# Rearranging the first two attentions of an attention-and-experts kernel

## The chip, the cores and the metric

The kernel runs on one core of a Trainium2 chip. A core has five engines that run side by side and wait for each other through semaphores: TensorE (matmuls; PE in the profile, PEld for its weight loads), VectorE (DVE), ScalarE (ACT), GpSimd (POOL) and SyncE (SP, which here only starts transfers). Each engine takes its own instructions in program order, so an instruction that has to wait holds up everything behind it on that engine, and nothing on the others. The metric is the time of one execution on the device in microseconds (us). Before the change it is 366.86 us, the median of three runs from 366.44 to 367.07.

## What is computed

Eight batches of grouped attention are followed by a mixture of experts with a two-level gate. Cut to what matters:

```python
# q (8, 16, 384, 64), k and v (8, 4, 384, 64), all float32
k = np.repeat(k, 4, axis=1); v = np.repeat(v, 4, axis=1)
scores = 1/np.sqrt(64) * np.matmul(q, k.transpose(0, 1, 3, 2))
attn = np.exp(scores - np.max(scores, axis=-1, keepdims=True))
attn = attn / (np.sum(attn, axis=-1, keepdims=True) + 1e-09)
x = np.matmul(attn, v)                       # then reshaped to (3072, 1024)

g_logits = x @ w_group                       # 4 groups
g_idx = np.argmax(g_logits, axis=1)          # and its softmax weight g_w
for g in range(4):
    e_logits = xg @ w_expert[g]              # 4 experts in each group
    e_idx = np.argmax(e_logits, axis=1)      # and its softmax weight e_w
    for e in range(4):
        h = np.maximum(xg[mask_e] @ w1[g, e], 0.0)
        ye = h @ w2[g, e]
        out[tok_idx] = (g_w * e_w)[:, None] * ye
```

## The kernel before

The kernel goes through the batches one after another. It guesses, from the mean of v, which expert the batch will choose, fetches the weights of that expert early, and runs the batch through it. The gate then says which tokens did choose it; a loop at the end does whatever was missed. The attention of batch b + 1 overlaps the expert of batch b.

An attention has 4 groups (g) of 6 units (c), so 24 units (u). TensorE does the score matmuls of unit u + 2, then the value matmuls of unit u; ScalarE takes the exponential of each unit's scores from PSUM into a buffer `e` (13 of them go round). To get the sums of the exponentials, GpSimd adds units 0 and 1 and units 2 and 3 of each group, in place, and VectorE reduces what is left (`reduce`, four times a group). When a group is done its output is copied from PSUM to `xT`.

```python
        def add(self, eng, u):
            eng.tensor_add(out=self.e[u], in0=self.e[u], in1=self.e[u + 1])

        def reduce(self, g, n, u):

            def emit():
                if reds[self.b] is None:
                    reds[self.b] = gpool.tile([P, Hkv, NR, 2, NB], F32, name="red")
                nc.vector.tensor_reduce(
                    out=reds[self.b][:, g, n].rearrange("p t j -> p (t j)"),
                    in_=self.e[u].rearrange("p t (j x) -> p (t j) x", x=32),
                    axis=AX.X, op=ALU.add, apply_transpose=True)
            if self.held is None:
                emit()
            else:
                self.held.append(emit)

        def release(self):
            for emit in self.held:
                emit()
            self.held = None

        def tail(self, u):
            b = self.b
            g, c = u // NC, u % NC
            z = u - c
            if c in (1, 3) and (b, u) != (1, 3):
                self.add(nc.gpsimd, u - 1)
            if (b, g) == (2, 0):
                for n in ((), (1,), (2, 0))[max(c, 3) - 3]:
                    self.reduce(g, n, (z, z + 4, z + 5)[n])
            elif c >= 3:
                self.reduce(g, c - 3, (z, z + 4, z + 5)[c - 3])
            if c == NC - 1:
                self.reduce(g, NR - 1, z + 2)
                if b not in xT:
                    # ... (makes xT[b]; for batch 1 in the room of a weight tile)
                dst, src = xT[b][:, KG * g:KG * (g + 1), :], self.oT[g][:, :, :S]
                if b > 1 and g < Hkv - 1 or (b, g) == (1, 1):
                    nc.vector.tensor_copy(out=dst, in_=src)
                else:
                    nc.scalar.copy(out=dst, in_=src)

        def run(self, u0, u1, inserts, nxt=None):
            for u in range(u0, u1):
                if u + 2 < NU:
                    self.score(u + 2)
                elif nxt is not None:
                    nxt.score(u + 2 - NU)
                self.pv(u)
                self.tail(u)
                for f in inserts.get(u, []):
                    f()
```

`collect` puts the four partial sums of a group together, `sums` sends them through TensorE to a PSUM tile and takes the reciprocal of what comes back, `spread` brings the reciprocals to the layout of `xT`, `scale_x` multiplies, and `cast` makes the bfloat16 copy that the expert reads. The PSUM tile "x" is the one of the two "o" tiles that the running group does not use; the next group takes it.

```python
    def collect(b, g0, g1):
        if b not in rsum:
            rsum[b] = gpool.tile([P, Hkv, 2, NB], F32, name="rsum")
        nc.vector.tensor_reduce(
            out=rsum[b][:, g0:g1].rearrange("p g t j -> p g (t j)"),
            in_=reds[b][:, g0:g1].rearrange("p g n t j -> p g (t j) n"), axis=AX.X, op=ALU.add)

    def sums(b, g0, g1, pt):
        if isinstance(pt, str):
            pt = ps_tile(pt)
        sm = pt[:, 1, 128:128 + Hkv * KG * NB].rearrange("p (g r j) -> p g r j", r=KG, j=NB)
        for r in range(2):
            for t in range(2):
                nc.tensor.matmul(out=sm[t * D:(t + 1) * D, g0:g1, r, :], lhsT=half32[:, r, :],
                                 rhs=rsum[b][:, g0:g1, t, :], start=True, stop=True)
        if b not in inv:
            inv[b] = gpool.tile([P, KQ, NB], F32, name="inv")
        nc.vector.reciprocal(out=inv[b][:, KG * g0:KG * g1],
                             in_=sm[:, g0:g1].rearrange("p g r j -> p (g r) j"))

    def spread(b, m, which=None):

        rb = gpool.tile([P, 2, S], F32, name="rb", bufs=2) if which is None else ps_tile(which)[:, :, :S]
        for r in range(2):
            nc.vector.transpose(
                out=rb[:, r].rearrange("p (j x) -> p j x", x=32),
                in_=inv[b][:, 2 * m + r].unsqueeze(2).to_broadcast([P, NB, 32]))
        return rb

    def scale_x(b, m, rb, eng):
        # ... (makes xb[b])
        x = xT[b][:, 2 * m:2 * m + 2, :]
        eng.tensor_mul(out=x, in0=x, in1=rb)

    def normalise(b, m, which=None):
        scale_x(b, m, spread(b, m, which), nc.vector)

    def cast(b, m, eng=None):
        ks = slice(2 * m, 2 * m + 2)
        evac(eng or nc.scalar, xb[b][:, ks, :], xT[b][:, ks, :])
```

The guess needs the sum of v over the positions (`sum_v`: one reduction on VectorE, or three additions on GpSimd), then a mean and two small matmuls, a chain of small VectorE operations that picks the expert (`pick_index`, cut here), and a read of the index into a GpSimd register (`pick`):

```python
    def sum_v(b, eng):
        vsum[b] = gpool.tile([P, Hkv, D], BF16, name="vsum")
        # on VectorE: one tensor_reduce over the positions of vraw[b] (line 461)
        # on GpSimd: three tensor_adds, 768, 256 and 256 wide (lines 467 to 469; in the diff)

    def pick_index(b):
        # ...
        nc.vector.tensor_scalar(oh1, key, km, None, op0=ALU.is_ge)     # line 580
        # ...

    def pick(b):
        ers[b] = nc.gpsimd.value_load(e_is[b][0:1, 0:1], min_val=0, max_val=NE - 1)

    def pick_w1(b):
        w1s[b] = fetch1(ers[b])

    def pick_w2(b):
        w2s[b] = fetch2(ers[b])

    # ffn_h: 16 matmuls for 256 columns of the hidden layer (in the diff)

    def first_fetch():
        pick(0)
        transposed(1)
        pick_w1(0)
```

The schedule of the first two attentions lists what is put in after which unit. `hold` keeps back the reductions of attention 1 until `release`:

```python
    GB = KG * SC
    a = at[0]
    a.run(0, NU, {
        1: [do(first_q, GB, GB, "x", nc.vector)],
        3: [cast_k],
        4: [gate_matrix_b, do(sum_v, 0, nc.gpsimd)],
        6: [do(collect, 0, 0, 1)],
        7: [do(first_q, 2 * GB, 2 * GB, "x", nc.vector)],
        8: [do(first_k, 1, "x", nc.vector)],
        10: [do(sums, 0, 0, 1, "x"), do(normalise, 0, 0)],
        13: [first_guess],
        14: [do(cast, 0, 0)],
        15: [do(collect, 0, 1, 2), first_pick],
        19: [first_fetch, do(sums, 0, 1, 2, "x")],
        20: [first_spread],
        21: [first_scale],
    }, at[1])
    collect(0, 2, Hkv)

    FU = 16
    a = at[1]
    hold(a)
    a.run(0, FU, {
        4: [do(sums, 0, 2, Hkv, "x")],
        5: [second_scale, do(a.add, nc.gpsimd, 2), do(pick_w2, 0), do(sum_v, 1, nc.vector)],
        6: [do(normalise, 0, 3, "x")],
        9: [do(load_k, 2), do(load_q, 2), do(cast, 0, 2)],
        11: [a.release, do(collect, 1, 0, 2), do(cast, 0, 3)],
    })
    moe_h(0, 0, "s")        # first of four expert tiles of batch 0
    # ... the rest of this stretch is in the diff
    a.run(FU, NU, {21: [do(sum_v, 2, nc.gpsimd)]})

    def first_block():
        prefetch(1)
        collect(1, 2, Hkv)
        weights[0]()
        out_weights(0)
        cast(1, 0)
        cast(1, 1)
        moe_y(0, 0, "s")
        sums(1, 2, Hkv, "o")
        normalise(1, 2)
        normalise(1, 3)
        moe_y(0, 1, "s")
        cast(1, 2)
        # ... rest of batch 0, then attention 2
```

Of the kernel before, what the change touches and what calls it, by code (L numbers as in the profile page):

```python
# [18 lines left out]
def kernel(  # L19
# [11 lines left out]
    nc = tc.nc  # L31
# [262 lines left out]
    class Attn:  # L294
# [62 lines left out]
        def tail(self, u):  # L357
            b = self.b
            g, c = u // NC, u % NC
            z = u - c  # L360
            if c in (1, 3) and (b, u) != (1, 3):
                self.add(nc.gpsimd, u - 1)
            if (b, g) == (2, 0):
                for n in ((), (1,), (2, 0))[max(c, 3) - 3]:
                    self.reduce(g, n, (z, z + 4, z + 5)[n])
            elif c >= 3:
                self.reduce(g, c - 3, (z, z + 4, z + 5)[c - 3])
            if c == NC - 1:
                self.reduce(g, NR - 1, z + 2)
                if b not in xT:  # L370
                    if b == 1:
                        w = wpool.tile([P, KQ, F], BF16, name="w1")
                        xT[b] = w.rearrange("p a f -> p (a f)").bitcast(F32)[
                            :, :KQ * S].rearrange("p (a n) -> p a n", n=S)
                    else:
                        xT[b] = xpool.tile([P, KQ, S], F32, name="xT", bufs=1)
                dst, src = xT[b][:, KG * g:KG * (g + 1), :], self.oT[g][:, :, :S]
                if b > 1 and g < Hkv - 1 or (b, g) == (1, 1):
                    nc.vector.tensor_copy(out=dst, in_=src)  # L379
                else:  # L380
                    nc.scalar.copy(out=dst, in_=src)  # L381

# [71 lines left out]
    vsum = {}  # L454

    def sum_v(b, eng):

        vsum[b] = gpool.tile([P, Hkv, D], BF16, name="vsum")
        with nc.allow_low_precision("only serves a guess"):
            if eng is nc.vector:  # L460
# [3 lines left out]
            n = NC // 2 * D  # L464
            t = gpool.tile([P, 2, S], F32, name="rb", bufs=2).rearrange(
                "p a s -> p (a s)").rearrange("p (g n) -> p g n", g=Hkv)
            eng.tensor_add(out=t, in0=vraw[b][:, :, :n], in1=vraw[b][:, :, n:])
# [150 lines left out]
    def ffn_h(x, w1, hT, f0, which, mid=None):  # L618
        h = ps_tile(which)
        for jj in range(2):  # L620
            for kq in range(KQ):
                nc.tensor.matmul(out=h[:, jj, :S], lhsT=w1[:, kq, (f0 + jj) * P:(f0 + jj + 1) * P],  # L622
                                 rhs=x[:, kq, :], start=(kq == 0), stop=(kq == KQ - 1))
            if mid is not None and jj == 0:
                mid()
# [23 lines left out]
    def moe_h(b, f0, which, mid=None):  # L649
        if f0 == 0:  # L650
            hTs[b] = xpool.tile([P, FQ, S], BF16, name="hT", bufs=1)
        ffn_h(xb[b], w1s[b], hTs[b], f0, which, mid)
# [48 lines left out]
    def first_fetch():  # L701
        pick(0)
        transposed(1)
        pick_w1(0)
# [21 lines left out]
    def second_scale():  # L726
# [7 lines left out]
        4: [gate_matrix_b, do(sum_v, 0, nc.gpsimd)],  # L734
# [3 lines left out]
        10: [do(sums, 0, 0, 1, "x"), do(normalise, 0, 0)],  # L738
        13: [first_guess],
        14: [do(cast, 0, 0)],  # L740
        15: [do(collect, 0, 1, 2), first_pick],
        19: [first_fetch, do(sums, 0, 1, 2, "x")],
# [9 lines left out]
        4: [do(sums, 0, 2, Hkv, "x")],  # L752
        5: [second_scale, do(a.add, nc.gpsimd, 2), do(pick_w2, 0), do(sum_v, 1, nc.vector)],
        6: [do(normalise, 0, 3, "x")],
        9: [do(load_k, 2), do(load_q, 2), do(cast, 0, 2)],
        11: [a.release, do(collect, 1, 0, 2), do(cast, 0, 3)],
    })
    moe_h(0, 0, "s")
# [4 lines left out]
    guess_mean(1, pt)  # L763
    vm = mean_copy(pt, nc.scalar)
    moe_h(0, 2, "s", do(sums, 1, 0, 2, pt))
    guess_logits(vm, pt)
    for m in range(2):
        normalise(1, m)
    moe_h(0, 4, "s")
    weights[0] = gate_softmax(0, pt, True)  # L770
    pick_index(1)
    moe_h(0, 6, "s")
    a.run(FU, NU, {21: [do(sum_v, 2, nc.gpsimd)]})

    def first_block():

        prefetch(1)
        collect(1, 2, Hkv)
# [212 lines left out]
```

The softmax here doesn't subtract the row's maximum and nothing guards it: scores larger than these inputs give would overflow.

## Time and profile before

| | before |
|---|---|
| time, median of 3 runs | 366.86 us |
| span of the profiled execution | 366.1 us |
| mean granted TensorE clock | 0.998 |
| TensorE / VectorE / ScalarE / GpSimd busy | 354.2 / 275.7 / 230.2 / 160.5 us |

The stretch that the change touches, from the table of busy time in stretches of 10 us (TensorE, VectorE, ScalarE and GpSimd, in us of 10):

| us | PE | DVE | ACT | POOL |
|---|---|---|---|---|
| 0 to 10 | 8.46 | 5.12 | 5.54 | 6.38 |
| 10 to 20 | 9.88 | 6.46 | 7.80 | 8.40 |
| 20 to 30 | 9.17 | 9.56 | 8.89 | 7.54 |
| 30 to 40 | 8.47 | 9.31 | 8.17 | 7.86 |
| 40 to 50 | 9.13 | 9.93 | 9.18 | 9.09 |
| 50 to 60 | 10.00 | 8.71 | 2.34 | 5.42 |
| 60 to 70 | 9.81 | 8.72 | 7.08 | 4.35 |
| 70 to 80 | 10.00 | 7.38 | 5.52 | 6.11 |

Attention 0 runs from about 7 to 33 us, units 0 to 15 of attention 1 from there to 50, the first half of batch 0's expert to 62.7, and the last 8 units of attention 1 to 69.4.

In the lines of a timeline the columns are the start, the time from start to end of the piece, the engine, the kernel's line, the operation, what it writes and reads with shapes, and how many instructions stand in the piece. In brackets behind it is the idle time of that engine ahead of the piece and what ended it. In the list of waits a line gives the engine and line that waited, what it waited for, and the total, the number and the longest of these waits. TensorE's matmuls overlap, and their ends are modelled, so starts are the safer thing to read.

### The profile page before, as it was taken

What the parts mean: (1) busy time and instruction counts of PE and PEld (TensorE: products, weight loads), DVE (VectorE), ACT (ScalarE), POOL (GpSimd) and SP (SyncE); (2) the same over time, 40 slices, a digit from 0 to 9 for tenths busy, and PEclk for the clock granted to TensorE, in tenths of its full rate; (3) what the DMA queues carried; (4) which work ended last, traced back from release to release, by engine and by line L of the source; (5) the groups of instructions that cost most, each with busy time, mean ns of one, the idle gap of its engine ahead of it and who ended that gap; (6) DMA issues with size and microseconds to landing.
All of it is one profiled execution on the core that took longest, in us unless ns stands there. A gap on an engine that the chain in (4) does not pass through costs nothing.

```text
span 366.1 us, 9424 instructions
## 1 busy us (share of the span) xinstructions
PE 354.2 (97%) x3907; PEld 183.2 (50%) x3907; DVE 275.7 (75%) x506; ACT 230.2 (63%) x300; POOL 160.5 (44%) x127
## 2 busy tenths in 40 slices
PE   8999899999999999999999999999999999999992
PEld 4544455445455455554455445554545545555641
DVE  5689998858988498867989579884998659892230
ACT  5789853759926597267954599265972679544221
POOL 6886890736811476033730377113760258300000
PEclk9999999999999999999999999999999999999999
DMA  8973999999998999999999999989999899999333
GB/s 188 251 118 57 194 181 220 156 208 253 224 163 173 216 252 211 148 209 238 232 208 148 205 249 212 192 175 216 252 210 137 151 211 234 212 213 240 90 85 93
DMA packets 69902, 69.79 MB, mean 191 GB/s; under 512 B 35832, under 2 KB 49944, under 8 KB 69856
## 3 DMA queue, kind: packets, MB, share of 16 engines
q0 software_dynamic: 26864, 41.81, 65.1%
q1 hardware_dynamic: 42320, 26.40, 31.2%
q10 hardware_dynamic: 672, 0.93, 0.9%
q8 instruction: 32, 0.52, 0.5%
q14 instruction: 14, 0.11, 0.1%
HBM read 89.21 MB, written 12.58 MB: 278 GB/s over the span
## 4 chain that ended last, share of the span: by engine, by line
PE 87%; DVE 5%; ACT 2%; POOL 1%; issue 1%; DMA 1%; ACTq 0%
PE ps_o L329 28%; PE ps_s L622 22%; PE ps_s L633 13%; PE ps_s L310 8%; PE ps_o L633 7%; PE ps_o L451 3%; DVE red L343 3%; ACT e L316 2%; PE ps_s L896 2%; PE ps_o L622 1%; POOL e L336 1%; PE ps_o L896 1%; DMA w<-in_q_dram 1%; PE ps_o L415 1%; DVE rb L426 1%
## 5 line engine op out<-in xcount | busy, mean ns | idle before, releaser
L316 ACT ACTIVATE e<-ps_s 128x768 f32<-128x768 f32 x192 | 150.7, 815 | 20.1 <-PE ps_s L310 16.2
L329 PE MATMUL ps_o<-e,v_raw 64*64 64x384 f32 x1536 | 153.3, 483 | 1.4 <-DVE inv L419 1.4
L336 POOL TENSOR_TENSOR e<-e 128x768 f32<-128x768 f32 x64 | 116.4, 1836 | 62.6 <-ACT e L316 43.8
L343 DVE TRANSPOSE_TENSOR_REDUCE red<-e 128x24 f32<-128x768 f32 x128 | 114.1, 946 | 18.3 <-POOL e L336 18.3
L622 PE MATMUL ps_s<-xb,w 128*128 128x384 bf16 x480 | 81.0, 326 | 0.5 <-ACT e L316 0.5
L329 PEld LDWEIGHTS ps_o<-e,v_raw 64*64 64x64 f32 x1536 | 55.4, 133 | 39.7 <-issue 27.4
L622 PEld LDWEIGHTS <-w 128*128 128x128 bf16 x512 | 48.9, 98 | 36.2 <-issue 4.7
L310 PE MATMUL ps_s<-qT,kT 64*64 64x384 bf16 x768 | 63.7, 326 | 0.7 <-ACT e L316 0.2
L626 ACT ACTIVATE hT<-ps_s 128x768 bf16<-128x768 f32 x30 | 24.3, 811 | 61.0 <-PE ps_s L622 58.0
L633 PE MATMUL ps_s<-w,hT 128*128 128x512 bf16 x224 | 50.6, 379 | 0.0
L633 PEld LDWEIGHTS <-hT 128*128 128x128 bf16 x336 | 31.3, 97 | 36.6 <-issue 2.1
L310 PEld LDWEIGHTS <-kT 64*64 64x64 bf16 x768 | 24.2, 105 | 38.9 <-issue 37.1
L689 POOL COPY after<-qT 128x1 bf16<-128x1 bf16 x7 | 2.1, 304 | 79.5 <-DMA qT<-q_raw 78.1
L426 DVE STREAM_TRANSPOSE rb<-inv 128x384 f32<-128x384 f32 x62 | 32.0, 555 | 0.4
L658 ACT ACTIVATE ot<-ps_s,we 128x1024 f32<-128x1024 f32 x14 | 15.6, 1115 | 25.5 <-PE ps_s L633 12.1
L633 PE MATMUL ps_o<-w,hT 128*128 128x512 bf16 x112 | 26.5, 379 | 0.0
L435 DVE TENSOR_TENSOR xT<-xT,rb 128x768 f32<-128x768 f32 x25 | 24.0, 958 | 0.9
L245 ACT CAST xb<-xT 128x768 bf16<-128x768 f32 x27 | 21.7, 830 | 0.0
L461 DVE TENSOR_REDUCE vsum<-v_raw 128x256 bf16<-128x1536 f32 x6 | 16.9, 2815 | 0.0
L379 DVE COPY xT<-ps_o 128x768 f32<-128x768 f32 x18 | 16.5, 919 | 0.0
L660 DVE TENSOR_SCALAR ot<-ps_o,we 128x1024 f32<-128x1024 f32 x7 | 9.0, 1282 | 5.6 <-PE ps_o L633 4.6
L381 ACT COPY xT<-ps_o 128x768 f32<-128x768 f32 x10 | 8.0, 799 | 6.6 <-PE ps_o L329 6.6
(129 smaller groups left out, 201.4 us busy)
## 6 DMA issues: line engine op xcount, KB each, us to landing
w<-in_moe_w_dram POOLq DMA_DIRECT2D x16, 2048.0 KB, 23.4
out_dram<-ot SPq DMA_DIRECT2D x42, 256.0 KB, 6.6
q_raw<-in_q_dram POOLq DMA_DIRECT2D x7, 768.0 KB, 32.1
v_raw<-in_v_dram SPq DMA_DIRECT2D x12, 384.0 KB, 5.3
k<-in_k_dram POOLq DMA_DIRECT2D x7, 192.0 KB, 28.9
out_dram<-ot SPq DMA_DIRECT2D x7, 128.0 KB, 2.3
v_raw<-in_v_dram POOLq DMA_DIRECT2D x2, 384.0 KB, 11.5
w<-in_q_dram POOLq DMA_DIRECT2D x3, 192.0 KB, 7.5
```

The lines of the kernel that those rows point to most:

```text
L245: eng.copy(out=out_, in_=in_)
L310: nc.tensor.matmul(out=sT[r * H2:(r + 1) * H2, s, :S], lhsT=kT[b][s * D:(s + 1) * D, slot, ks], rhs=qT[b][s * D:(s + 1) * D, kq * SC:(kq + ...
L316: nc.scalar.activation(e.rearrange("p t (s x) -> p s t x", s=2), sT[:, :, :S].rearrange("p s (t x) -> p s t x", t=2), ACT.Exp, scale=scale)
L329: nc.tensor.matmul(out=oT[t * D:(t + 1) * D, r, :S], lhsT=vraw[b][r * H2:(r + 1) * H2, g, c * D:(c + 1) * D], rhs=self.e[u][r * H2:(r + 1) ...
L336: eng.tensor_add(out=self.e[u], in0=self.e[u], in1=self.e[u + 1])
L343: nc.vector.tensor_reduce(out=reds[self.b][:, g, n].rearrange("p t j -> p (t j)"), in_=self.e[u].rearrange("p t (j x) -> p (t j) x", x=32) ...
L426: nc.vector.transpose(out=rb[:, r].rearrange("p (j x) -> p j x", x=32), in_=inv[b][:, 2 * m + r].unsqueeze(2).to_broadcast([P, NB, 32]))
L435: eng.tensor_mul(out=x, in0=x, in1=rb)
L461: eng.tensor_reduce(out=vsum[b], in_=vraw[b].rearrange("p g (c d) -> p g d c", d=D), axis=AX.X, op=ALU.add)
L622: nc.tensor.matmul(out=h[:, jj, :S], lhsT=w1[:, kq, (f0 + jj) * P:(f0 + jj + 1) * P], rhs=x[:, kq, :], start=(kq == 0), stop=(kq == KQ - 1))
L626: nc.scalar.activation(hT[:, f0:f0 + 2, :], h[:, :, :S], ACT.Relu)
L633: nc.tensor.matmul(out=y[:, nh, :], lhsT=hT[:, f, c * P:(c + 1) * P], rhs=w2[:, f, nh * HALF:(nh + 1) * HALF], start=(f == 0), stop=(f == ...
```

## The change

It rearranges the work of the engines beside TensorE in attentions 0 and 1; the matmuls are the same in number and shape. Batch 0's sum of v on GpSimd is cut in two, so that additions of exponentials come between its parts; batch 1's goes from VectorE to GpSimd, behind the last additions ahead of the expert. The index of batch 0's expert is read ahead of the addition of units 18 and 19. The PSUM copies of attention 0's group 3 and attention 1's groups 0 and 2 go from ScalarE to VectorE, and in group 1 of attention 1 the copy goes ahead of the reductions. The last three reductions of group 2 in attention 1 are done at the pause for the expert, as their exponentials are there by then. The reductions of attention 1 are released after unit 8 in place of 11. Two casts leave the run of exponentials; they now come ahead of the first expert tile, whose matmuls are reordered to read the parts of `x` in the order in which they become ready. Sums, mean and guess of batch 1 come one expert tile later, and its `pick_index` after attention 1.

```diff
@@ -357,16 +357,12 @@
         def tail(self, u):
             b = self.b
             g, c = u // NC, u % NC
-            z = u - c
-            if c in (1, 3) and (b, u) != (1, 3):
+            if c in (1, 3):
                 self.add(nc.gpsimd, u - 1)
-            if (b, g) == (2, 0):
-                for n in ((), (1,), (2, 0))[max(c, 3) - 3]:
-                    self.reduce(g, n, (z, z + 4, z + 5)[n])
-            elif c >= 3:
-                self.reduce(g, c - 3, (z, z + 4, z + 5)[c - 3])
+            sums_first = (b, g) != (1, 1)
+            if sums_first or c < NC - 1:
+                self.reductions(g, c)
             if c == NC - 1:
-                self.reduce(g, NR - 1, z + 2)
                 if b not in xT:
                     if b == 1:
                         w = wpool.tile([P, KQ, F], BF16, name="w1")
@@ -375,10 +371,25 @@
                     else:
                         xT[b] = xpool.tile([P, KQ, S], F32, name="xT", bufs=1)
                 dst, src = xT[b][:, KG * g:KG * (g + 1), :], self.oT[g][:, :, :S]
-                if b > 1 and g < Hkv - 1 or (b, g) == (1, 1):
+                if b > 0 and g < Hkv - 1 or (b, g) == (0, Hkv - 1):
                     nc.vector.tensor_copy(out=dst, in_=src)
                 else:
                     nc.scalar.copy(out=dst, in_=src)
+                if not sums_first:
+                    self.reductions(g, c)
+
+        def reductions(self, g, c):
+
+            b, z = self.b, g * NC
+            if (b, g) == (1, 2) and c > 3:
+                return
+            if (b, g) == (2, 0):
+                for n in ((), (1,), (2, 0))[max(c, 3) - 3]:
+                    self.reduce(g, n, (z, z + 4, z + 5)[n])
+            elif c >= 3:
+                self.reduce(g, c - 3, (z, z + 4, z + 5)[c - 3])
+            if c == NC - 1:
+                self.reduce(g, NR - 1, z + 2)
 
         def start(self):
             self.score(0)
@@ -451,7 +462,7 @@
                 nc.tensor.matmul(out=pt[32 * t:32 * t + 32, 0, :32 * SC], lhsT=wg[:, kq, :],
                                  rhs=x[:, t], start=(kq == 0), stop=(kq == KQ - 1))
 
-    vsum = {}
+    vsum, vhalf = {}, {}
 
     def sum_v(b, eng):
 
@@ -461,10 +472,21 @@
                 eng.tensor_reduce(out=vsum[b], in_=vraw[b].rearrange("p g (c d) -> p g d c", d=D),
                                   axis=AX.X, op=ALU.add)
                 return
-            n = NC // 2 * D
-            t = gpool.tile([P, 2, S], F32, name="rb", bufs=2).rearrange(
-                "p a s -> p (a s)").rearrange("p (g n) -> p g n", g=Hkv)
-            eng.tensor_add(out=t, in0=vraw[b][:, :, :n], in1=vraw[b][:, :, n:])
+        sum_v_halves(b, eng)
+        sum_v_rest(b, eng)
+
+    def sum_v_halves(b, eng):
+        n = NC // 2 * D
+        t = gpool.tile([P, 2, S], F32, name="rb", bufs=2).rearrange(
+            "p a s -> p (a s)").rearrange("p (g n) -> p g n", g=Hkv)
+        eng.tensor_add(out=t, in0=vraw[b][:, :, :n], in1=vraw[b][:, :, n:])
+        vhalf[b] = t
+
+    def sum_v_rest(b, eng):
+        t = vhalf[b]
+        if b not in vsum:
+            vsum[b] = gpool.tile([P, Hkv, D], BF16, name="vsum")
+        with nc.allow_low_precision("only serves a guess"):
             eng.tensor_add(out=t[:, :, :D], in0=t[:, :, :D], in1=t[:, :, D:2 * D])
             eng.tensor_add(out=vsum[b], in0=t[:, :, :D], in1=t[:, :, 2 * D:])
 
@@ -615,14 +637,17 @@
             j = 2 * c + h
             yield slice(h * H2, (h + 1) * H2), 2 * (j % SC) + j // SC
 
-    def ffn_h(x, w1, hT, f0, which, mid=None):
+    def ffn_h(x, w1, hT, f0, which, mid=None, split=False):
         h = ps_tile(which)
-        for jj in range(2):
-            for kq in range(KQ):
-                nc.tensor.matmul(out=h[:, jj, :S], lhsT=w1[:, kq, (f0 + jj) * P:(f0 + jj + 1) * P],
-                                 rhs=x[:, kq, :], start=(kq == 0), stop=(kq == KQ - 1))
-            if mid is not None and jj == 0:
-                mid()
+        cuts = (0, KQ - 2 * KG, KQ - KG, KQ) if split else (0, KQ)
+        for k0, k1 in zip(cuts, cuts[1:]):
+            for jj in range(2):
+                for kq in range(k0, k1):
+                    nc.tensor.matmul(out=h[:, jj, :S],
+                                     lhsT=w1[:, kq, (f0 + jj) * P:(f0 + jj + 1) * P],
+                                     rhs=x[:, kq, :], start=(kq == 0), stop=(kq == KQ - 1))
+                if mid is not None and jj == 0 and k0 == 0:
+                    mid()
         nc.scalar.activation(hT[:, f0:f0 + 2, :], h[:, :, :S], ACT.Relu)
 
     def ffn_y(w2, hT, c, which, nhs=(0, 1), y=None, fs=None):
@@ -646,10 +671,10 @@
 
     hTs = {}
 
-    def moe_h(b, f0, which, mid=None):
+    def moe_h(b, f0, which, mid=None, split=False):
         if f0 == 0:
             hTs[b] = xpool.tile([P, FQ, S], BF16, name="hT", bufs=1)
-        ffn_h(xb[b], w1s[b], hTs[b], f0, which, mid)
+        ffn_h(xb[b], w1s[b], hTs[b], f0, which, mid, split)
 
     def y_out(b, c, y, eng=None):
         ot = opool.tile([P, DM], F32, name="ot")
@@ -699,7 +724,6 @@
         pick_index(0)
 
     def first_fetch():
-        pick(0)
         transposed(1)
         pick_w1(0)
 
@@ -731,14 +755,17 @@
     a.run(0, NU, {
         1: [do(first_q, GB, GB, "x", nc.vector)],
         3: [cast_k],
-        4: [gate_matrix_b, do(sum_v, 0, nc.gpsimd)],
+        4: [gate_matrix_b],
+        5: [do(sum_v_halves, 0, nc.gpsimd)],
         6: [do(collect, 0, 0, 1)],
         7: [do(first_q, 2 * GB, 2 * GB, "x", nc.vector)],
         8: [do(first_k, 1, "x", nc.vector)],
         10: [do(sums, 0, 0, 1, "x"), do(normalise, 0, 0)],
+        11: [do(sum_v_rest, 0, nc.gpsimd)],
         13: [first_guess],
         14: [do(cast, 0, 0)],
         15: [do(collect, 0, 1, 2), first_pick],
+        16: [do(pick, 0)],
         19: [first_fetch, do(sums, 0, 1, 2, "x")],
         20: [first_spread],
         21: [first_scale],
@@ -749,33 +776,42 @@
     a = at[1]
     hold(a)
     a.run(0, FU, {
-        4: [do(sums, 0, 2, Hkv, "x")],
-        5: [second_scale, do(a.add, nc.gpsimd, 2), do(pick_w2, 0), do(sum_v, 1, nc.vector)],
+        5: [do(sums, 0, 2, Hkv, "x"), second_scale, do(pick_w2, 0)],
         6: [do(normalise, 0, 3, "x")],
-        9: [do(load_k, 2), do(load_q, 2), do(cast, 0, 2)],
-        11: [a.release, do(collect, 1, 0, 2), do(cast, 0, 3)],
+        8: [a.release],
+        9: [do(load_k, 2), do(load_q, 2)],
+        11: [do(collect, 1, 0, 2)],
     })
-    moe_h(0, 0, "s")
+    sum_v(1, nc.gpsimd)
+    for n, u in ((1, FU), (2, FU + 1), (3, FU - 2)):
+        a.reduce(2, n, u)
+    for m in range(2, Hkv):
+        cast(0, m)
+    moe_h(0, 0, "s", split=True)
     load_v(2, nc.gpsimd)
     transposes(2)
     pt = ps_tile("x")
     gate_logits(0, pt)
-    guess_mean(1, pt)
-    vm = mean_copy(pt, nc.scalar)
-    moe_h(0, 2, "s", do(sums, 1, 0, 2, pt))
-    guess_logits(vm, pt)
+    moe_h(0, 2, "s")
+    moe_h(0, 4, "s", do(sums, 1, 0, 2, pt))
     for m in range(2):
         normalise(1, m)
-    moe_h(0, 4, "s")
+
+    def second_mean():
+        guess_mean(1, pt)
+        state["vm"] = mean_copy(pt, nc.scalar)
+
+    moe_h(0, 6, "s", second_mean)
+    guess_logits(state["vm"], pt)
     weights[0] = gate_softmax(0, pt, True)
-    pick_index(1)
-    moe_h(0, 6, "s")
-    a.run(FU, NU, {21: [do(sum_v, 2, nc.gpsimd)]})
+    a.run(FU, NU, {})
+    sum_v(2, nc.gpsimd)
 
     def first_block():
 
+        collect(1, 2, Hkv)
+        pick_index(1)
         prefetch(1)
-        collect(1, 2, Hkv)
         weights[0]()
         out_weights(0)
         cast(1, 0)
```

## The prediction

> **What bounds the kernel now.** I read the page's busy rows first, then the waits of TensorE up to 70 us, then the timelines of single engines there.
>
> ```profile
> PE 354.2 (97%) x3907; PEld 183.2 (50%) x3907; DVE 275.7 (75%) x506; ACT 230.2 (63%) x300; POOL 160.5 (44%) x127
> PE   8999899999999999999999999999999999999992
> ```
>
> TensorE is busy 97% of the span, and its holes lie early. From 70 us on, the table of stretches has it busy throughout. The change touches only attentions 0 and 1 and the expert work between them, which end near 84 us, and it removes no matmul. It can only close holes. The waits of TensorE from 0 to 70 us:
>
> ```profile
> PE ps_o L329 <- DVE inv L419: 1.4, 2, 0.8
> ...
> PE ps_o L415 <- DVE rsum L405: 0.9, 1, 0.9
> PE ps_s L622 <- ACT e L316: 0.5, 1, 0.5
> ...
> PE ps_s L310 <- ACT e L316: 0.2, 1, 0.2
> ```
>
> These add to 3.0 us, but part of the loss looks busy. Undisturbed, one attention unit (4 score and 8 value matmuls) starts 0.81 us after the last. TensorE's timeline gives the excess:
>
> ```profile
> 22.14 0.88 PE L329 MATMUL ps_o<-e,v_raw 64*64 64x384 f32 x8 [0.83 <-DVE inv L419]
> ...
> 33.80 0.88 PE L329 MATMUL ps_o<-e,v_raw 64*64 64x384 f32 x8 [0.61 <-DVE inv L419]
> ...
> 38.82 0.42 PE L415 MATMUL ps_o<-rsum,half 128*64 128x24 f32 x8 [0.92 <-DVE rsum L405]
> ...
> 49.91 2.27 PE L622 MATMUL ps_s<-xb,w 128*128 128x384 bf16 x13 [0.53 <-ACT e L316]
> ...
> 66.29 0.36 PE L310 MATMUL ps_s<-qT,kT 64*64 64x384 bf16 x4 [0.19 <-ACT e L316]
> ```
>
> Read each start against the value matmuls before it. **Hole 1**: 20.34 + 0.81 = 21.15, actual 22.14: 0.99 lost. **Hole 2**: 32.21 + 0.81 = 33.02, actual 33.80: 0.78. **Hole 3**: 0.92 at the sums. **Hole 4**: starts at 42.06, 45.77, 47.73 and 49.91 lose 0.28, 0.48, 0.29 and about 0.55, together 1.6. **Hole 5**: starts at 63.65 and 66.46 lose 0.14 and 0.40. With 0.1 of crumbs, the ceiling of any rearrangement here is about 4.9 us (1.3%).
>
> Holes 1 to 3 are VectorE's lateness: a PSUM tile used for the sums of exponentials isn't free until its reciprocal is read, or its input isn't collected. VectorE has almost no idle time from 20 to 53 us. Hole 4 is ScalarE's:
>
> ```profile
> 43.82 0.85 ACT L245 CAST xb<-xT 128x768 bf16<-128x768 f32 x1
> 44.54 1.55 ACT L316 ACTIVATE e<-ps_s 128x768 f32<-128x768 f32 x2
> 45.93 0.87 ACT L245 CAST xb<-xT 128x768 bf16<-128x768 f32 x1
> 46.65 1.56 ACT L316 ACTIVATE e<-ps_s 128x768 f32<-128x768 f32 x2
> 49.04 1.51 ACT L316 ACTIVATE e<-ps_s 128x768 f32<-128x768 f32 x2 [0.82 <-POOL e L336]
> ```
>
> An exponential takes about 0.73 at pitch, only 0.08 under TensorE's unit, so each cast or copy among them (0.7 to 0.8) stops the scores. The last line waits for the exponential buffer that a GpSimd add frees.
>
> **What the skill says.** The Trainium skill, "Perfetto Trace Analysis", section "Optimization Strategy": look for the gaps of the bounding engine and for the instruction that ends each. That is the route above. "GPSIMD Engine Reference", section "1. Specifications": GpSimd has no access to PSUM; so PSUM copies can go only to ScalarE or VectorE, as all of them do in this trace. "SBUF — State Buffer", section "SBUF: two separate sides": VectorE and GpSimd share a port pair under an exclusive lock, held for a whole instruction; VectorE needs it for two SBUF inputs (against a GpSimd op that reads SBUF) or a two-port mode. The trace agrees (VectorE, VectorE, GpSimd):
>
> ```profile
> 28.92 1.62 DVE L580 TENSOR_SCALAR oh_all<-key,km 128x16 f32<-128x16 f32 x1
> 63.27 0.23 DVE L580 TENSOR_SCALAR oh_all<-key,km 128x16 f32<-128x16 f32 x1
> 28.69 1.82 POOL L336 TENSOR_TENSOR e<-e 128x768 f32<-128x768 f32 x1 [1.06 <-ACT xT L381]
> ```
>
> The same tiny instruction takes 0.23 with GpSimd quiet and 1.62 beside an add, and ends as the add ends (30.54 and 30.51).
>
> **The change part by part.** Shifts are of TensorE's clock against before.
>
> (a) *v summed between adds.* The GpSimd sum is 1.83 + 0.73 + 0.73, about 3.4 us in one piece from 14.81. Now only the first 1.83 stands ahead of group 1's add: that add starts at 16.64 instead of 18.20 and ends at 18.47. VectorE's reduction of it (at 20.06 after 1.32 idle) can follow the key copy that ends at 18.74. The reciprocal moves from 21.82 to about 20.5, before TensorE wants the tile at 21.15. Hole 1 closes: **-0.99**, and VectorE is 1.3 ahead.
>
> (b) *pick read ahead of an add.* GpSimd waits for the index before the add of group 3, so no add runs beside the choice chain and L580 takes 0.23: 1.39 saved. The chain ends at 30.94 - 1.32 - 1.39 = 28.2, the three reductions behind it at 30.8, the reciprocal at 31.1. TensorE wants the tile at 33.02 - 0.99 - 0.1 = 31.9. Hole 2 closes: **-0.78**, and crumbs -0.1. GpSimd's read takes 0.95 (30.94 to 31.89 before), so the add runs from 29.15 instead of 28.69, later but not in the way; the weights are asked for 0.8 earlier.
>
> (c) *PSUM copies to VectorE, sums one unit later.* VectorE gains two copies of 0.95 ahead of the reciprocal of groups 2 and 3. Its queue: reciprocal 31.1, spread to 32.0, four reductions (the last waits for a GpSimd add until about 34.5) to 35.6, copy to 36.5, collect to 36.95, copy of attention 1's group 0 to 37.9, reciprocal to 38.3. The sums now come after unit 5, when TensorE wants them at about 36.75; it waits about 0.2 for collect. Unit 6 needs that PSUM tile again, so it starts at 38.4 instead of 37.25. The loss is about 1.1 where hole 3 lost 0.9: **+0.2**. Shift now about -1.7.
>
> (d) *ScalarE relieved.* From 34 to 47 us it loses a copy and two casts, 2.3 us. VectorE's sum of v (2.88) goes to GpSimd, and the held reductions are released 3 units earlier. So TensorE runs at 0.81 from unit 6 at 38.4. One brake is left: unit 15's exponential takes the buffer that the add of units 6 and 7 frees. GpSimd's queue (two adds from about 37.1, scaling 1.85, a 0.95 issue, that add) ends it at 45.4; ScalarE wants it at 44.5, TensorE loses 0.5. The expert's first matmul starts near 47.1 instead of 49.9: **-1.1** (1.6 less 0.5). Weights asked for at 32.7 need about 11 (traffic after the old request at 33.5 falls off near 45), so they are there by 44.
>
> (e) *First expert tile split.* The two casts now follow the last exponentials, about 47.7 to 49.2, while 8 of 16 matmuls (1.3 us) run on the first two groups. The third group is wanted at 48.4 and cast at 48.5, the fourth at 49.2 and cast at 49.3: **+0.2**.
>
> (f) *Sums of group 2 ahead, copy (1,2) to VectorE.* VectorE does three reductions (2.69) at 51 to 54 us, where it would wait for the sums anyway. ScalarE's copy at 64.72 (0.82) leaves the exponentials and closes the larger part of hole 5: **-0.4**. The 0.14 behind the last Relu stays.
>
> Sum: -0.99 - 0.78 - 0.1 + 0.2 - 1.1 + 0.2 - 0.4 = **-3.0**. I give back 0.1 for (g): the last normalisations, done at 77.8, leave 1.9 of slack before the gate matmuls at 78.59 need them. TensorE comes 3.0 earlier, VectorE about 1.4, because index and weights now run beside the GpSimd sum of attention 2's v. 366.86 - 2.9 is 364.0.
>
> **Rivals.** *The wait only moves.* In (c) copies, collect and reciprocal stand in one row ahead of unit 6. If VectorE isn't the 1.3 us ahead that (a) and (b) give it, TensorE waits 2 us there and the gain shrinks to 1.5 to 2: about 365.2. For it: VectorE is full there. Against: both savings are read off the trace. *GpSimd becomes the bound.* It gains 3.3 us of adds and one add moves ahead; if every add after 37 us is 1 us later, unit 15 loses 1.5 and later buffers follow: about 365. *Transfers hide it.* From 74 us on the chip's transfers run in a ring: prefetch, transposes, GpSimd's check, next prefetch, at 73.8, 117.0, 159.4, 203.9 us, some 43 apart against TensorE's 42.74. If the ring doesn't start earlier, it takes the gain. Against: weights asked for at 74.44 land 19.6 later, near 94, and are used at 101.71, so 3 us off leaves over 4. If it did bite: about 366. *The lock bites elsewhere* (in (g)): another 0.5 to 1, about 364.8.
>
> **Range and chances.** All holes closed gives 366.86 - 4.9 = 362.0, which needs (c), (d) and (e) without any wait; half of that ceiling is 364.4, and the rivals lie at 365 to 366. I take 364.0, with 362.9 to 365.7. A 2% gain would need 359.5, beyond the ceiling: chance 0.01. A 2% loss would need 7.3 us of new waits, more than the holes there are now: 0.01.
>
> **What would show it.** Right: no wait above 0.3 for the reciprocal at 21 and 31 us; L580 at 0.23 in the first pick; ScalarE without casts until about 47; the expert's first matmul near 47, the first output matmuls at 66 to 67 instead of 69.39. Wrong: a wait over 1.5 us of TensorE at unit 5 or 6 of attention 1; L580 still long; a wait at the gate matmuls near 75; TensorE waiting for weights after 95 us; or the end moving by much less than the first output matmul.

## The result and the profile after

The changed kernel takes 364.72 us, the median of four runs (364.27 to 365.54), against 366.72 for the kernel before beside it: a ratio of 0.9947, with a 95% interval from 0.9927 to 0.9968. Measured again with more runs of both on one chip it took 363.92 against 366.85, a ratio of 0.9918 (0.9902 to 0.9933). So the gain is real and small, 2.0 us in the first measurement and 2.9 in the second; the prediction said 2.9.

The page's first rows after the change:

```profile
span 362.0 us, 9409 instructions
PE 351.5 (97%) x3892; PEld 183.1 (51%) x3907; DVE 274.9 (76%) x508; ACT 229.2 (63%) x297; POOL 162.4 (45%) x130
PE   7999999999999999999999999999999999999992
```

No engine has much less to do. What has changed is the row of slices: the fifth, from about 37 to 46 us, was an 8 and is a 9. (The first, the start of the kernel, is a 7 for an 8.) (15 matmul records are missing from this trace, so TensorE's busy sum is somewhat low.) TensorE's waits from 0 to 70 us, six lines before, are three:

```profile
PE ps_o L277 <- DVE ones L155: 1.2, 1, 1.2
PE ps_o L329 <- DVE inv L430: 0.8, 1, 0.8
PE ps_o L262 <- DVE w L281: 0.5, 1, 0.5
```

The first and last belong to the start of the kernel. The middle one is new in place, not in kind: it stands at unit 6 of attention 1. TensorE's timeline at the places of the old holes:

```profile
20.21 0.81 PE L329 MATMUL ps_o<-e,v_raw 64*64 64x384 f32 x8
...
21.02 0.81 PE L329 MATMUL ps_o<-e,v_raw 64*64 64x384 f32 x8
...
31.16 0.81 PE L329 MATMUL ps_o<-e,v_raw 64*64 64x384 f32 x8
...
31.97 0.82 PE L329 MATMUL ps_o<-e,v_raw 64*64 64x384 f32 x8
...
36.00 0.81 PE L329 MATMUL ps_o<-e,v_raw 64*64 64x384 f32 x8
36.75 0.42 PE L426 MATMUL ps_o<-rsum,half 128*64 128x24 f32 x8
37.10 0.36 PE L310 MATMUL ps_s<-qT,kT 64*64 64x384 bf16 x4
38.27 0.88 PE L329 MATMUL ps_o<-e,v_raw 64*64 64x384 f32 x8 [0.82 <-DVE inv L430]
...
46.35 2.77 PE L646 MATMUL ps_s<-xb,w 128*128 128x384 bf16 x16
49.05 1.53 PE L462 MATMUL ps_o<-xT,wg 128*32 128x96 f32 x64
```

Holes 1 and 2 are gone: unit 12 (21.02) follows unit 11 (20.21) by 0.81, and attention 1 starts at 31.97, 0.81 after the unit at 31.16. The sums at 36.75 wait for nothing, but unit 6 behind them loses 1.0: it starts 2.27 after unit 5, where a unit with sums ahead of it that don't hold it up comes 1.3 after the last (27.44 and 28.74 in this trace). From unit 7 on the units come 0.81 apart, and the first expert tile's 16 matmuls run in one piece from 46.35.

**A measure that leaves the start out.** The first transfers land a little differently in each run: the first value matmul starts between 7.53 and 9.16 us in the 14 traces of this study. Therefore I compare the time from the first value matmul (line 329) to the first output matmul of batch 0 (line 633, or 658 after). It ends behind nearly all that the change touches. Counted from that first matmul, units ahead of the place that an edit changes start within 0.03 us of the same time in every trace of the changed kernel and its variants, so one trace places what an edit costs. The edits were timed on several chips; each time is therefore given with its ratio to the kernel before beside it, to be held against the changed kernel's 0.9947 and 0.9918. The times alone are too coarse for most of these edits; the traces decide.

| kernel | first value | first output | between | from there to the end of the span |
|---|---|---|---|---|
| before, first trace | 8.23 | 69.33 | 61.10 | 296.8 |
| before_again | 8.18 | 68.63 | 60.45 | 296.9 |
| changed, first trace | 8.11 | 65.34 | 57.23 | 296.7 |
| after_again | 7.81 | 65.05 | 57.24 | 297.1 |

### The profile page after: what moved, and what is told of

Read it like the earlier page. It is cut to its first block, busy times and chain, and to the rows that moved or that the text cites. A ratio compares the mean times of both kernels' runs of the same rounds, so it can differ in the third digit from the quotient of the medians.

```text
span 362.0 us, 9409 instructions
## 1 busy us (share of the span) xinstructions
PE 351.5 (97%) x3892; PEld 183.1 (51%) x3907; DVE 274.9 (76%) x508; ACT 229.2 (63%) x297; POOL 162.4 (45%) x130
## 4 chain that ended last, share of the span: by engine, by line
PE 95%; DMA 1%; DVE 1%; issue 0%; ACT 0%; ACTq 0%
PE ps_o L329 34%; PE ps_s L646 22%; PE ps_s L658 13%; PE ps_s L310 9%; PE ps_o L658 7%; PE ps_o L462 3%; PE ps_s L932 2%; PE ps_o L646 1%; PE ps_o L932 1%; DMA w<-in_q_dram 1%; PE ps_o L426 1%; PE ps_o L262 0%; PE ps_o L496 0%; DVE qT L247 0%; DVE w L375 0%
## 5 line engine op out<-in xcount | busy, mean ns | idle before, releaser
L658 PE MATMUL ps_s<-w,hT 128*128 128x512 bf16 x211 | 49.0, 379 | 0.9 <-issue 0.2
L714 POOL COPY after<-qT 128x1 bf16<-128x1 bf16 x7 | 1.3, 189 | 91.1 <-DMA qT<-q_raw 91.1
L375 DVE COPY xT<-ps_o 128x768 f32<-128x768 f32 x19 | 17.5, 919 | 0.0
L472 DVE TENSOR_REDUCE vsum<-v_raw 128x256 bf16<-128x1536 f32 x5 | 14.0, 2802 | 0.0
L518 DVE STREAM_TRANSPOSE gl<-ps_o 128x96 f32<-128x96 f32 x8 | 2.3, 282 | 12.6 <-PE ps_o L511 9.3
```

The costliest lines, as they stand in the source:

```text
L658: nc.tensor.matmul(out=y[:, nh, :], lhsT=hT[:, f, c * P:(c + 1) * P], rhs=w2[:, f, nh * HALF:(nh + 1) * HALF], start=(f == 0), stop=(f == ...
```

## The experiments

The theory was the prediction's: TensorE is the bound, time is lost only in its holes, and VectorE's row or ScalarE's run of exponentials makes each hole. The rivals: VectorE's lateness just moves from hole to hole; GpSimd or the buffers it frees make the holes; the transfers or the granted clock take the gain back after 70 us.

### Both kernels again

No edit.

> The kernel before, unchanged, profiled and timed anew. The first two traces differ by 4.1 us in span and by 4.05 us at the first output matmul (69.39 and 65.34), while the median times differ by 2.0. Theory H (the holes are the same in every run, and the trace of before was a late one in its launch only): first output matmul again near 69.4, time near 366.7. Rival V (the holes vary from run to run, and the first trace of before had more of them than a usual run): first output matmul near 67.5 to 68.5.

> The changed kernel, unchanged, profiled and timed anew. Theory H: first output matmul near 65.3 again, time near 364.7. Rival V: it may lie up to 1 us elsewhere. Rival T (the denser TensorE is granted a lower clock and pays part of the gain back after 84 us): mean clock below that of the kernel before by 0.002 or more, and the stretch from the first output matmul to the end longer than in the kernel before.

Measured: before_again 367.13 us (366.45 to 368.17), after_again 363.92 (363.47 to 364.32). Both theories on the traces are partly right. The changed kernel's stretch repeats to 0.01 us; that of the kernel before doesn't, and the difference of 0.65 is hole 1. This is a line of GpSimd's timeline in the first trace of before:

```profile
14.35 0.51 POOL L288 CAST w<-w 128x384 bf16<-128x384 f32 x1 [1.07 <-DMA w<-in_k_dram]
```

And the same line in the second trace, before_again:

```profile
13.59 0.51 POOL L288 CAST w<-w 128x384 bf16<-128x384 f32 x1 [0.38 <-DMA w<-in_k_dram]
```

There TensorE's unit 12 reads:

```profile
21.42 0.88 PE L329 MATMUL ps_o<-e,v_raw 64*64 64x384 f32 x8 [0.15 <-DVE inv L419]
```

Ahead of the sum of v GpSimd casts the second half of the keys. In the first trace it waited 1.07 for them to land, in the second 0.38. Everything behind it on GpSimd, then on VectorE, shifted by that, and hole 1 was 0.99 in the one and 0.32 in the other (21.42 against 20.29 + 0.81). From hole 1 on the two traces agree within 0.03. The stretch to the end is the same in both kernels within 0.4 and has no order. The granted clock lay between 0.993 and 0.998 in both kernels, except for one run of the kernel before at 0.991, which took 369.95 us; the trace of after_again with 0.993 has a span of 362.1, and runs of it at 0.998 have 361.7 to 362.2. That rules out the clock and the ring of transfers as takers of the gain.

### The index read after the add

```diff
-        16: [do(pick, 0)],
     def first_fetch():
+        pick(0)
         transposed(1)
```

> The changed kernel with the index read after the add of units 18 and 19 again. Lock theory: the comparison in the choice chain takes about 1.6 again, VectorE is 1.4 later from 28 us on; TensorE waits about 0.3 for the reciprocal ahead of attention 1 and some 1.4 more at unit 6 than now: first output matmul 1.2 to 1.5 later, time near 366.0. Rival (slack: the sum of v between the adds gave VectorE enough lead by itself): under 0.4 us.

Measured: 364.74 us (ratio 0.9950), 58.46 between: 1.22 more than the changed kernel, as the lock theory has it, but the lock fell elsewhere. VectorE's timeline in this run:

```profile
26.81 0.23 DVE L602 TENSOR_SCALAR oh_all<-key,km 128x16 f32<-128x16 f32 x1
27.08 1.83 DVE L605 SCALAR_TENSOR_TENSOR t<-eidx,oh_all 128x16 f32<-128x16 f32 x1
```

GpSimd's beside it:

```profile
27.06 1.81 POOL L336 TENSOR_TENSOR e<-e 128x768 f32<-128x768 f32 x1 [1.55 <-ACT e L316]
```

And VectorE's in the changed kernel:

```profile
27.39 0.23 DVE L602 TENSOR_SCALAR oh_all<-key,km 128x16 f32<-128x16 f32 x1
27.65 0.17 DVE L605 SCALAR_TENSOR_TENSOR t<-eidx,oh_all 128x16 f32<-128x16 f32 x1
```

The add started 0.02 before line 605, which reads two SBUF operands, and held it until its own end (28.87, against 28.91). The comparison just ahead got through. So it is not one operation that is slow; whichever needs the pair first after the add starts pays for all of it. TensorE paid at three places:

```profile
31.95 0.88 PE L329 MATMUL ps_o<-e,v_raw 64*64 64x384 f32 x8 [0.40 <-DVE inv L430]
37.69 0.42 PE L426 MATMUL ps_o<-rsum,half 128*64 128x24 f32 x8 [0.82 <-DVE rsum L416]
38.92 0.88 PE L329 MATMUL ps_o<-e,v_raw 64*64 64x384 f32 x8 [0.53 <-DVE inv L430]
```

One delay of 1.66 on VectorE comes back as waits of 0.40, 0.82 and 0.53, where the changed kernel has none, none and 0.82: VectorE has no idle time between them in which to catch up. By the starts TensorE loses 0.56 at the first of these places and 0.67 by unit 6: the delay is paid in parts, and the parts come to less than the delay.

### v in one piece, alone and with the late index read

```diff
-        4: [gate_matrix_b],
-        5: [do(sum_v_halves, 0, nc.gpsimd)],
+        4: [gate_matrix_b, do(sum_v, 0, nc.gpsimd)],
-        11: [do(sum_v_rest, 0, nc.gpsimd)],
```

The second kernel has the edit above as well.

> The changed kernel with batch 0's sum of v on GpSimd in one piece after unit 4 again. From the first value matmul to the first output matmul the changed kernel takes 57.24 us in both of its traces. Row theory: the add of units 6 and 7 ends about 1.5 later, VectorE is some 1.0 later, TensorE waits 0.5 at unit 12 of attention 0 and 0.3 to 0.5 more at unit 6 of attention 1: 58.0 to 58.3. Rival (the pick alone gives VectorE the lead it needs): 57.7 to 57.8, the loss at unit 12 alone.

> The changed kernel with both the sum of v in one piece and the index read after the add. Alone they cost 0.20 and 1.22 from first value to first output matmul (57.44 and 58.46 against 57.24). Row theory (each covers for the other, as VectorE has about 1 us of lead before the wait ahead of attention 1): more than the sum of both, 58.8 to 59.4. Rival (the losses just add, or overlap): 58.4 to 58.7.

Measured: 364.43 us (0.9924) and 57.44 between for the first, 365.97 (0.9979) and 59.58 for the second. The first fell below both expectations: only 0.20. In it the keys came early (GpSimd waited 0.33), unit 12 lost 0.24, and at unit 6 only 0.05 was added to the 1.0 that the changed kernel loses there anyway. In the second run the keys came late, with a wait of 1.04 on GpSimd:

```profile
13.99 0.51 POOL L288 CAST w<-w 128x384 bf16<-128x384 f32 x1 [1.04 <-DMA w<-in_k_dram]
```

TensorE's unit 12 in it:

```profile
21.79 0.88 PE L329 MATMUL ps_o<-e,v_raw 64*64 64x384 f32 x8 [0.80 <-DVE inv L430]
```

The two edits cost 2.34 together, 0.92 more than 0.20 + 1.22. The starts say where: 0.97 is lost at unit 12 (0.24 in the first run), 0.78 ahead of attention 1 (0.56 in undo_pick) and 0.66 by unit 6 (0.67 there). So some 0.7 of the excess is the later landing (1.04 - 0.33), and 0.2 comes ahead of attention 1, where a lead lost to v in one piece would show. Only this 0.2, in one trace, speaks for the row theory.

What is shown: with v in one piece a late landing goes straight to TensorE. In the four traces that have it so, the waits of 1.07, 0.38, 0.33 and 1.04 go with losses at unit 12 of 0.99, 0.32, 0.24 and 0.97. With v in two pieces it doesn't: after_again had a wait of 0.67 there and no hole, and undo_casts (below) the longest of all, here GpSimd and then TensorE's unit 12:

```profile
13.91 0.51 POOL L288 CAST w<-w 128x384 bf16<-128x384 f32 x1 [1.13 <-DMA w<-in_k_dram]
```

```profile
20.67 0.81 PE L329 MATMUL ps_o<-e,v_raw 64*64 64x384 f32 x8
```

That is 12.91 after its first value matmul (7.76), as in the changed kernel (21.02 and 8.11).

### The PSUM copies back on ScalarE

```diff
-                if b > 0 and g < Hkv - 1 or (b, g) == (0, Hkv - 1):
+                if b > 1 and g < Hkv - 1 or (b, g) == (1, 1):
```

> The changed kernel with the three PSUM copies (group 3 of attention 0, groups 0 and 2 of attention 1) on ScalarE again. ScalarE theory: each copy stops the exponentials for 0.7 and TensorE for 0.3 to 0.6, while the wait at unit 6 shrinks from 1.0 to about 0.5: 57.7 to 58.2 from first value to first output matmul. Rival (ScalarE has the slack, and the copies only lengthen VectorE's row): 56.6 to 56.8, faster than the changed kernel.

Measured: 363.70 us (0.9916), 57.30 between: no difference from the changed kernel, and neither expectation. Its two waits show why:

```profile
38.00 0.88 PE L329 MATMUL ps_o<-e,v_raw 64*64 64x384 f32 x8 [0.27 <-DVE inv L430]
...
62.43 0.36 PE L310 MATMUL ps_s<-qT,kT 64*64 64x384 bf16 x4 [0.19 <-ACT e L316]
```

By the starts, the copies on ScalarE cost 0.23 in the first units of attention 1 and 0.39 at unit 20 (the line at 62.43, hole 5 as before), and off VectorE's row they give back 0.52 at unit 6. With the sums where the change puts them, moving all three copies is an exchange. The places suggest that the copy of group 2 alone gains 0.4 on VectorE while the other two lose 0.3 there; a kernel that moves only that one was not run.

### The casts among the exponentials

```diff
-        9: [do(load_k, 2), do(load_q, 2)],
-        11: [do(collect, 1, 0, 2)],
+        9: [do(load_k, 2), do(load_q, 2), do(cast, 0, 2)],
+        11: [do(collect, 1, 0, 2), do(cast, 0, 3)],
-    for m in range(2, Hkv):
-        cast(0, m)
```

> The changed kernel with the two casts of batch 0 among the exponentials again (after units 9 and 11), the split first expert tile kept. ScalarE theory: the second half of hole 4 comes back, 0.8 to 1.4: 58.0 to 58.6 from first value to first output matmul. Rival (the release of buffers by GpSimd and VectorE was the cause of hole 4): under 0.3.

Measured: 365.00 us (0.9942), 58.33 between, 1.09 more. TensorE in this run:

```profile
43.22 0.36 PE L310 MATMUL ps_s<-qT,kT 64*64 64x384 bf16 x4 [0.39 <-ACT e L316]
...
45.36 0.36 PE L310 MATMUL ps_s<-qT,kT 64*64 64x384 bf16 x4 [0.33 <-ACT e L316]
```

Each cast makes the scores wait for a PSUM tile once. The ScalarE theory stands for this part.

### The release after unit 11

```diff
-        8: [a.release],
-        11: [do(collect, 1, 0, 2)],
+        11: [a.release, do(collect, 1, 0, 2)],
```

> The changed kernel with the held reductions of attention 1 released after unit 11 instead of 8. They then start about 2.6 later on VectorE, and the buffers that the exponentials of units 16 and 17 take come free near 45 and 46, about when ScalarE wants them. Buffer theory (hole 4 of the kernel before was in part a wait for buffers): 57.6 to 58.2 from first value to first output matmul. Rival (there is slack): under 57.4.

Measured: 365.14 us (0.9950), 58.23 between, 0.99 more, so the buffer theory holds beside the casts. ScalarE's timeline:

```profile
45.71 1.51 ACT L316 ACTIVATE e<-ps_s 128x768 f32<-128x768 f32 x2 [0.97 <-POOL e L336]
```

TensorE's:

```profile
46.57 2.96 PE L646 MATMUL ps_s<-xb,w 128*128 128x384 bf16 x16 [0.74 <-ACT e L316]
```

Unit 16's exponential waits for a GpSimd add, as it did before the change (0.82), and not for the reductions that were made late. Unit 15's waits 0.25 for the add ahead of that one, of units 6 and 7, which costs TensorE nothing. In the changed kernel neither waits: unit 15's exponential starts at 44.20, before the add of units 6 and 7 ends there (near 44.45), so it has another buffer. The place of the release decides which buffers these two get. By what rule buffers are handed out is not shown, as the profile doesn't name them.

### The first expert tile in one run

```diff
-    moe_h(0, 0, "s", split=True)
+    moe_h(0, 0, "s")
```

> The changed kernel with the 16 matmuls of the first expert tile in their old order, over all of x for one half and then the other. The casts still end some 1.8 after the tile's start. If the order matters, TensorE waits for both casts in its first half: 57.8 to 58.1 from first value to first output matmul. If VectorE or the gate sets what follows anyway: no more than 57.4.

Measured: 364.55 us (0.9939), 58.03 between, 0.79 more.

```profile
45.77 0.82 PE L646 MATMUL ps_s<-xb,w 128*128 128x384 bf16 x4
46.82 0.48 PE L646 MATMUL ps_s<-xb,w 128*128 128x384 bf16 x2 [0.23 <-ACT xb L245]
47.55 1.79 PE L646 MATMUL ps_s<-xb,w 128*128 128x384 bf16 x10 [0.25 <-ACT xb L245]
```

Four matmuls run on what is ready, two on each cast's result, and the rest on all of it. The same work in the changed order has no wait at all. So the late casts are worth 1.09 only because the order of the matmuls hides them; in the old order 0.79 of it is lost again.

### Batch 1's sum of v on VectorE

```diff
-        5: [do(sums, 0, 2, Hkv, "x"), second_scale, do(pick_w2, 0)],
+        5: [do(sums, 0, 2, Hkv, "x"), second_scale, do(pick_w2, 0), do(sum_v, 1, nc.vector)],
-    sum_v(1, nc.gpsimd)
```

> The changed kernel with batch 1's sum of v as one reduction on VectorE after unit 5 again (GpSimd loses 3.3 of adds). VectorE theory: everything behind it on VectorE is 2.8 later, the copy of attention 1's group 1 ends near 50, and TensorE waits about 1 for that tile at the gate matmuls: 58.0 to 58.5 from first value to first output matmul. Rival (VectorE has 1.7 of idle time near 54 and the sum fits in): under 57.5.

Measured: 365.71 us (0.9954), 58.46 between, 1.22 more. The size was expected, but the place was not:

```profile
45.30 0.88 PE L329 MATMUL ps_o<-e,v_raw 64*64 64x384 f32 x8 [0.92 <-DVE xT L446]
```

That is unit 12, which wants the PSUM tile in which the reciprocals of the last group are spread; with 2.90 more ahead of it the multiplication that reads them ends at 45.24. At the gate matmuls about 0.1 is lost.

### The sums later still

The hole that is left at unit 6 comes from a tile: after unit 5 the spare tile is the one that unit 6 takes. One unit later the spare tile is that of the group just finished.

```diff
-        5: [do(sums, 0, 2, Hkv, "x"), second_scale, do(pick_w2, 0)],
-        6: [do(normalise, 0, 3, "x")],
+        6: [do(sums, 0, 2, Hkv, "x"), second_scale, do(pick_w2, 0), do(normalise, 0, 3, "x")],
```

sums_u7 is the same with 7 for 6.

> The changed kernel with the sums of groups 2 and 3 after unit 6 of attention 1 in place of unit 5, so that their tile is that of the finished group and TensorE needn't wait for the reciprocal at unit 6. Theory H: the wait of 0.82 at 38.27 goes, about 1.0 us, first output matmul near 64.3, time near 363.7. Rival R (the transfers' ring or the clock sets the end now): the first output matmul moves the same, but the time stays within 0.3 of the changed kernel's.

> The changed kernel with the sums of groups 2 and 3, the scaling behind them and the normalisation of group 3 after unit 7. With them after unit 6 a wait of 0.28 for the copy of group 0 was left. If VectorE and GpSimd still finish the scaled groups before the casts at the first expert tile: that wait goes too, 56.2 to 56.3 from first value to first output matmul, time 362.7. If the later scaling comes late for the casts: 56.6 or more.

Measured: sums_u6 363.03 us (362.89 to 363.04), 56.52 between, a ratio to the kernel before of 0.9891 (0.9875 to 0.9908). sums_u7 363.36 us (362.71 to 364.27), 56.75 between, 0.9898 (0.9881 to 0.9915). One line of TensorE for each, sums_u6 first:

```profile
38.01 0.42 PE L426 MATMUL ps_o<-rsum,half 128*64 128x24 f32 x8 [0.28 <-DVE w L375]
```

```profile
42.84 0.88 PE L329 MATMUL ps_o<-e,v_raw 64*64 64x384 f32 x8 [0.21 <-DVE xT L446]
```

After unit 6, the sums wait 0.28 for the copy of group 0 out of that tile; the 1.0 becomes 0.3, and the time falls with it. After unit 7 that wait is gone too, but now unit 12 waits for the multiplication that reads the tile, and that and the expert tile lose 0.5 where 0.3 was won. Both traces have a shorter stretch than the changed kernel, and sums_u6's slowest run (363.04) is faster than the fastest of after_again (363.47), timed beside it. By its trace it is the best version here; the times of the two can't be told apart.

## Why the prediction was right

It was right in its sum and in most of its mechanism; several of its terms were off and made up for each other, which is luck. Against the first trace of before, step by step, each stretch read from start to start:

| step | predicted | measured | what the runs say |
|---|---|---|---|
| (a) sum of v between adds | -0.99 | -0.99 or -0.32 | depends on when the keys land |
| (b) index ahead of the add, and crumbs | -0.88 | -0.7 | -0.78 at hole 2, no crumbs; undoing it costs 1.22 |
| (c) copies and sums | +0.2 | -0.1 | hole 3 for a new wait of 1.0 at unit 6 |
| (d) ScalarE relieved | -1.1 | -1.7 | the brake of 0.5 didn't show |
| (e) split tile | +0.2 | 0.0 | no wait; unsplit it would be +0.8 |
| (f) sums ahead, copy of attention 1's group 2 | -0.4 | -0.43 | hole 5 gone but for 0.1; undo_copies brings 0.39 of it back |
| (g) last normalisations | +0.1 | 0.0 | gate matmuls 9.19 after the first output matmul in both |

Up to the first output matmul the first pair of traces gives -3.9 in all, where -3.0 was predicted. In the second pair (before_again and after_again) (a) is -0.32, every other step is the same within 0.03, and the sum is -3.2. The first output matmul, forecast at 66 to 67, came at 65.34 and 65.05; the other signs of being right showed as named. Doing the sums of group 2 ahead, the other half of (f), was not undone by itself.

*(a) was read from one trace as if it were the kernel's.* The 1.07 of waiting for keys stood in that trace, in GpSimd's timeline, and made most of hole 1. Against before_again the change gives 3.2 between first value and first output, not the 3.9 that the first traces show.

*(b)* VectorE's lock was rightly named. The price was put at hole 2 alone (0.78), while taking it back costs 1.22, because a late VectorE holds TensorE up again at unit 6; the first rival had named that place. The 0.5 to 1 that rival four gave to the lock near 68 us was not paid: two instructions were slowed there, to 0.37 and 0.56 (0.17 and 0.23 unhindered), and the gate matmuls didn't wait.

*(c)* Predicted: sums waiting 0.2, unit 6 at 38.4. Measured: no wait and 38.27. The new wait is the one as foretold; the sign differs because hole 3, put at 0.92 from the wait, was 1.0 by the starts. What the prediction didn't see is that with this place of the sums the three copies together are worth nothing (undo_copies), and that one unit later most of the wait goes.

*(d)* The brake was to be the add of units 6 and 7, ending at 45.4, whose buffer unit 15's exponential would take. GpSimd ended it near 44.45, as its queue began 0.7 earlier than predicted (36.36 for 37.1), and unit 15's exponential had started at 44.20 without it. In the trace, units 7 to 15 come at 0.81 without a gap. The step named the early release but left unit 15 with that buffer; with the late release (undo_release) the wait for it is there, and the release as a whole is worth 0.99.

The rivals: the wait did move, to 1.0 us and not to 2. GpSimd didn't become the bound, and transfers hid nothing: 296.3 to 297.1 us follow the first output matmul in all 14 traces.

The first measurement's gain of 2.0 is less than either pair of traces gives. The traced executions of the first pair were not typical: that of the kernel before took 367.74 us, more than any of its timed runs there (366.44 to 367.07), and that of the changed kernel 364.27, the fastest of its four. A prediction read from such a trace counts too much for (a); that (d) was worth 0.6 more than thought hides it.

## What to carry to other kernels

When one engine is busy to 97%, read the starts of its equal pieces for holes, since waits alone showed 3.0 of 4.9 us here, and take any hole that ends at a transfer from more than one trace. A helper engine without idle time gives one delay back in parts, at the places where it is next needed, so price it over all of them. Before moving work off an engine, look at which buffer or tile the waiting instruction needs: the place of one line (which tile is spare after which unit, which buffer comes free in time) was worth 0.7 us for the sums and 1.0 for the release.

## What the runs showed of the hardware

The Trainium skill, "SBUF — State Buffer", section "SBUF: two separate sides", says that a VectorE instruction with two SBUF inputs, or in a two-port mode, and a GpSimd instruction that reads SBUF exclude each other for a whole instruction, whichever starts first. The runs agree, and show how long that is for a tiny one: 1.62 for a comparison that takes 0.23, and 1.83 for a line of 16 elements that takes 0.17, when it starts 0.02 after an add of 1.81. It works the other way too: a GpSimd add of 1.82 took 2.65 when it started together with a VectorE multiplication of two SBUF tiles of 0.96 (at 23.19 in the trace of before). Four VectorE reductions with a transpose (128x768, about 0.88 each, from 31.82 in the changed kernel) kept their pace beside such an add.
